# A mixed-layer kernel (FFT filter, then soft MoE): the first DFT stage as float32 on four 64x64 tiles, over sums and differences of token pairs

## The chip, the core and the metric

The kernel runs on one core of one Trainium2 chip. The core has a matmul engine (TensorE, PE in the profile, with its weight loads as PEld), a vector engine (VectorE, DVE), a scalar engine (ScalarE, ACT), GpSimd (POOL) and SyncE (SP), which in this kernel issues every DMA. The metric is the device time of one execution in microseconds (us). Three timed executions of the kernel before took 419.14, 420.32 and 425.69 us; the median, 420.32 us, is the time before.

## The reference

The input is 8 sequences of 2496 tokens with 256 channels. Each channel is filtered in the frequency domain, and the result goes through a soft mixture of experts (8 experts of 4 slots each).

```python
X = np.fft.rfft(x, axis=1)                      # x: (8, 2496, 256)
y = np.fft.irfft(X * (filt_r + 1j * filt_i)[None], n=2496, axis=1)
x = y.reshape(19968, 256)
logits = x @ phi                                # (19968, 32)
d = softmax(logits, axis=0)                     # dispatch, over the tokens (its sum + 1e-9)
slot_input = d.T @ x                            # 32 x 256
for e in range(8):                              # four slots each
    slot_out[e] = np.maximum(slot_input[e] @ w1[e], 0) @ w2[e]
c = softmax(logits, axis=1)                     # combine, over the slots
return c @ slot_out
```

## The kernel before

The DFT of 2496 points is split as 39 x 64 (`N1`, `N2`). A first stage takes, for each of the 64 residues, a DFT over 39 tokens and keeps 20 of the 39 frequencies (`NT`), since x is real. A second stage multiplies by the 64-point matrices.

**First stage** (`split_x`, `s1_unit`). x is laid out on the host so that 3 residues of 39 tokens (117 rows, `KR`) lie on the partitions. One unit is two such columns, 512 numbers wide; a batch has 11 units (`NH`). A unit of batches 1 to 7 is split into a high and a low part: ACT rounds x to `xh` (line 297), POOL makes `xl = x - xh` (line 298), and PE adds three matmuls in the format float32r into one PSUM bank (line 311), with the block-diagonal matrix `w1h` or `w1l`, 117 rows by 120 columns (3 residues x 20 frequencies x real and imaginary part). Batch 0 takes one float32 matmul for each unit (line 308). The PSUM pool `ps_s1` has two banks, one unit each. The result is copied to SBUF as `at` by ACT (line 315; in batch 0 every second by DVE, line 313) and stored to DRAM (`a_dram`, line 319).

**Second stage** (`load_ash`, `x_unit`). The store to DRAM and the load back (`ash`, line 332) turn the layout: 64 residues x real and imaginary part come to lie on the 128 partitions. A batch has ten slots of two frequencies: four float32 matmuls of 128 columns (line 342), the filter on DVE and POOL (lines 355 to 359), and two slots later four transposes (line 369) and their copy `y` (line 371); the logits' spectrum follows (line 380).

**Chains** (`chain`). When the last batch of a group is through, a chain of smaller steps turns the logits' spectrum back into logits (lines 413 to 460), takes the softmax over tokens (line 492), transforms the weights (lines 509 to 557) and adds up the slots' inputs (line 584). Two of its steps are issued with each slot.

**Order.** The loop over 80 slots (8 batches x 10) issues, for slot n, the load of `ash` five slots ahead (`ASH`), the second stage of n, the first-stage units that `at_slot` gives to n (those of the next batch, five slots early, `AHEAD`), the transposes of n - 2 and two chain steps. From this the framework's scheduler makes a fixed order for each engine. SP has one queue, in which a DMA that waits for a buffer, for a copy or for the eighth DMA before it holds up everything behind. Before slot 0 lie batch 0's first stage and the loads of the filter tables, spread by the string `STEPS`. After the slots come the last chains, the experts (lines 819 to 845) and the output (`blocks`, lines 908 and 917).

## Time and profile before

The profiled execution took 419.54 us; its span, from the first to the last instruction, was 417.4 us at a mean granted TensorE clock of 0.967.

| engine | busy us | share of the span |
|---|---|---|
| PE, matmuls | 370.9 | 89% |
| PE, weight loads | 284.1 | 68% |
| DVE | 271.2 | 65% |
| ACT | 218.3 | 52% |
| POOL | 201.6 | 48% |
| DMA queue of SP | 106.26 MB moved | 79.4% of 16 engines |

Busy time is the union of an engine's instructions; matmuls are pipelined, so a busy PE isn't PE at its peak. The stages lie one behind the other: until 39 us the front (x of batch 0, tables, its first stage), from 39 to 292 us the 80 slots, with first-stage units until 234 us, until 340 us the last chains, then the experts and the output. Shares mean little over the whole span, so the stages are read apart.

### The profile page before, as it was taken

To read this page: it belongs to the slowest core of one execution; us is meant where nothing else is said; L and a number is where in the kernel's file an instruction comes from. 1 tells how busy PE (TensorE), PEld (TensorE's weight loads), DVE (VectorE), ACT (ScalarE), POOL (GpSimd) and SP (SyncE) were. 2 spreads that over 40 slices of the span, in tenths; PEclk is the share of its full clock that TensorE was granted. 3 is DMA by queue.
4 is the path that set the end of the run, shared out by engine and by line. 5 is a ranking of instruction groups with operands and counts; after the bars stand their busy time and mean duration, and the time that the engine had idled before them with its cause. 6 is when DMAs were issued, how large, how long until landed. Compare 5 with 4: busy or idle time off the path is not lost.

```text
span 417.4 us, 12612 instructions
## 1 busy us (share of the span) xinstructions
PE 370.9 (89%) x5049; PEld 284.1 (68%) x5049; DVE 271.2 (65%) x495; ACT 218.3 (52%) x474; POOL 201.6 (48%) x234
## 2 busy tenths in 40 slices
PE   8667898999999899999997999998998889989940
PEld 3235676888878787887886678888676634688830
DVE  1341672987889973878999475899259522487740
ACT  2376557675667845676685434444255411376630
POOL 0027669798769564967786225666021200433100
PEclk9688999999999999999999999999999999999985
DMA  8999999999969978797996543442169899199996
GB/s 215 232 302 292 311 303 326 344 303 339 295 197 347 300 223 236 215 269 193 276 285 207 169 152 85 121 130 77 53 201 379 282 296 321 49 415 410 417 417 279
DMA packets 61084, 107.07 MB, mean 256 GB/s; under 512 B 6046, under 2 KB 37662, under 8 KB 58850
## 3 DMA queue, kind: packets, MB, share of 16 engines
q1 hardware_dynamic: 61026, 106.26, 79.4%
q8 instruction: 40, 0.66, 0.6%
q14 instruction: 18, 0.15, 0.1%
HBM read 63.50 MB, written 42.74 MB: 255 GB/s over the span
## 4 chain that ended last, share of the span: by engine, by line
PE 59%; DMA 18%; DVE 11%; ACT 4%; issue 3%; SPq 1%; POOL 1%; ACTq 0%; DVEq 0%; POOLq 0%
PE x L342 14%; PE s L311 7%; DMA xt<-in_x 7%; PE t L369 6%; PE out L908 5%; PE s L584 4%; DMA ash<-a_dram 4%; PE l L380 4%; DMA out<-ob 3%; PE v L426 3%; PE dt L540 2%; DVE t L356 2%; PE lg L453 2%; PE s L308 2%; PE h L819 2%
## 5 line engine op out<-in xcount | busy, mean ns | idle before, releaser
L298 POOL TENSOR_TENSOR xl<-xt,xh 117x512 fp32r<-117x512 f32 x77 | 102.6, 1345 | 54.2 <-ACT xh L297 49.6
L342 PE MATMUL x<-b_t,ash 128*128 128x128 f32 x640 | 90.0, 281 | 7.7 <-DMA ash<-a_dram 4.6
L342 PEld LDWEIGHTS x<-b_t,ash 128*128 128x128 f32 x640 | 79.8, 191 | 18.8 <-issue 7.0
L359 POOL TENSOR_TENSOR yt<-yt,t 128x256 f32<-128x256 f32 x80 | 65.8, 825 | 40.2 <-DVE t L356 30.9
L355 DVE TENSOR_TENSOR yt<-x,fr_t 128x512 f32<-128x512 f32 x80 | 54.7, 684 | 39.6 <-PE x L342 36.1
L297 ACT CAST xh<-xt 117x512 fp32r<-117x512 f32 x77 | 46.9, 623 | 36.7 <-DMA xt<-in_x 12.3
L371 ACT COPY y<-t 128x512 f32<-128x512 f32 x80 | 46.5, 591 | 34.5 <-PE t L369 28.7
L315 ACT COPY at<-s 120x512 f32<-120x512 f32 x83 | 48.3, 586 | 23.1 <-PE s L308 11.3
L356 DVE TENSOR_TENSOR t<-x,fi_t 128x512 f32<-128x512 f32 x80 | 54.3, 679 | 0.0
L369 PE MATMUL t<-cst_t,yt 128*128 128x128 f32 x320 | 48.5, 276 | 1.3 <-issue 0.7
L358 DVE TENSOR_TENSOR yt<-yt,t 128x256 f32<-128x256 f32 x60 | 44.8, 756 | 0.8
L369 PEld LDWEIGHTS t<-cst_t,yt 128*128 128x128 f32 x320 | 37.3, 141 | 8.5 <-issue 3.6
L311 PE MATMUL s<-xh,w1h 117*120 117x512 f32 x77 | 36.1, 469 | 3.9 <-ACT xh L297 3.6
L908 PE MATMUL out<-so_h,st 32*128 32x256 f32 x312 | 30.2, 300 | 3.8 <-ACT st L862 3.1
L311 PE MATMUL s<-xl,w1h 117*120 117x512 f32 x77 | 32.7, 424 | 0.2
L311 PE MATMUL s<-xh,w1l 117*120 117x512 f32 x77 | 31.3, 406 | 0.0
L358 POOL TENSOR_TENSOR yt<-yt,t 128x256 f32<-128x256 f32 x20 | 16.2, 808 | 30.6 <-DVE t L356 24.2
L917 DVE COPY ob<-out 128x512 f32<-128x512 f32 (+1 forms) x40 | 25.2, 672 | 6.3 <-PE out L908 5.1
L908 PEld LDWEIGHTS out<-so_h,st 32*128 32x128 f32 x312 | 24.0, 183 | 6.7 <-ACT st L862 3.5
L908 PE MATMUL out<-so_l,st 32*128 32x256 f32 x312 | 28.0, 277 | 0.0
L917 ACT COPY ob<-out 128x512 f32<-128x512 f32 (+1 forms) x40 | 21.3, 580 | 11.4 <-PE out L908 9.1
L380 PE MATMUL l<-yt,phi_t 128*32 128x128 f32 x640 | 26.1, 278 | 1.3 <-ACT y L371 1.2
(116 smaller groups left out, 552.9 us busy)
## 6 DMA issues: line engine op xcount, KB each, us to landing
ash<-a_dram SPq DMA_DIRECT2D x80, 256.0 KB
a_dram<-at SPq DMA_DIRECT2D x80, 240.0 KB
xt<-in_x SPq DMA_DIRECT2D x40, 448.0 KB
out<-ob SPq DMA_DIRECT2D x17, 1024.0 KB
w<-in_w SPq DMA_DIRECT2D x64, 256.0 KB
out<-ob SPq DMA_DIRECT2D x5, 512.0 KB
xt<-in_x SPq DMA_DIRECT2D x8, 224.0 KB
c_dram<-lg SPq DMA_DIRECT2D x2, 643.5 KB
```

Of the source, the lines that this page charges most:

```text
L297: act.copy(xh, xs)
L298: pool_e.tensor_tensor(out=xl, in0=xs, in1=xh.bitcast(F32), op=ALU.subtract)
L311: pe.matmul(ps, w, xx, start=(n == 0), stop=(n == 2))
L315: act.copy(at, ps)
L342: pe.matmul(ps[:, 2 * k + dh].rearrange("q r c -> q (r c)"), ash[:, k, dh * P : (dh + 1) * P], b_t[:, t0 + k, :], start=True, stop=True,)
L355: dve.tensor_tensor(out=yt, in0=ps, in1=frv, op=ALU.mult)
L356: dve.tensor_tensor(out=t2, in0=ps[:, :, ::-1, :], in1=fiv, op=ALU.mult)
L358: add.tensor_tensor(out=yt[:, :, 1, :], in0=yt[:, :, 1, :], in1=t2[:, :, 1, :], op=ALU.add)
L359: pool_e.tensor_tensor(out=yt[:, :, 0, :], in0=yt[:, :, 0, :], in1=t2[:, :, 0, :], op=ALU.subtract)
L369: pe.transpose(pt[:, k, dh, :], yt[:, c % 2, 2 * k + dh].rearrange("q r c -> q (r c)"), ident)
L371: act.copy(y, pt.rearrange("k p h d -> k p (h d)"))
L908: nc.tensor.matmul(prs[k][:, mm, :], st[q, n // 2, c0 : c0 + P], (so_h, so_l)[n % 2][q, :], start=(n == 0), stop=(n == 3),)
```

## The change

Every token pair s and 39 - s enters the real part through its sum and the imaginary part through its difference. The host now lays x out as 20 + 19 tokens side by side, the second in reverse; two residue groups (`h`) lie on partitions 0 to 63 and 64 to 127, 60 of 64 rows used, with zeros in the rest. `fold_x` makes the sums `e` (on DVE for batch 0, on POOL after it) and, in place, the differences (always POOL). The real part is a 60 x 60 matrix times `e`, the imaginary part a 60 x 60 matrix times the difference, both in float32. `s1_unit` issues four matmuls on the four quarters of the array: rows by `h`, columns by real or imaginary part. A unit now is two of the old ones; a batch has 6 (`NU`), the last half as wide. Its PSUM tile has two banks, one for each `h`, and `ps_s1` holds one such tile. The rounding on ACT and the split on POOL are gone. Each unit has two copies and four stores of 60 partitions, where two old units had two stores of 120. `a_dram` holds all real parts ahead of the imaginary ones, so the second stage's matrices have their rows reordered, and the copies of `minv` and `u` now turn that order on the way (strided reads). x is loaded in one DMA of 128 partitions where there were two (112 and 5). Four x tiles of one unit are held (`XB`), instead of three of two old units, and six half-unit `at` tiles (`AB`) instead of five of a unit.

```diff
-XC = 4
-XB = 3
-AB = 5
+XB = 4
+AB = 6
...
-        for lo, hi in ((0, RX), (RX, KR)):
-            sp.dma_start(t[lo:hi, 0:n, :], x[b, lo:hi, i0 : i0 + n, :])
-        xts[b, c] = t
+    def load_x(b, u):
         pool = x0p if b == 0 else proda
+        t = pool.tile([P, 2, 2, DIM], F32, tag="xt", name=f"xt{b}_{u}", bufs=6 if b == 0 else XB)
+        n = min(2, NH - 2 * u)
+        sp.dma_start(t[:, 0:n], x[b, :, 2 * u : 2 * u + n])
+        xts[b, u] = t
...
-        xh = proda.tile([KR, 2, DIM], F32R, tag="xh", name=f"xh{b}_{u}", bufs=3)
-        xl = proda.tile([KR, 2, DIM], F32R, tag="xl", name=f"xl{b}_{u}", bufs=3)
-        act.copy(xh, xs)
-        pool_e.tensor_tensor(out=xl, in0=xs, in1=xh.bitcast(F32), op=ALU.subtract)
-        xhl[b, u] = xh, xl
+    def fold_x(b, u):
+        n = min(2, NH - 2 * u)
+        xt = xts.pop((b, u))
+        e = proda.tile([P, 2, DIM], F32, tag="e", name=f"e{b}_{u}", bufs=3)
+        eng = dve if b == 0 else pool_e
+        eng.tensor_tensor(out=e[:, 0:n], in0=xt[:, 0:n, 0], in1=xt[:, 0:n, 1], op=ALU.add)
+        pool_e.tensor_tensor(out=xt[:, 0:n, 1], in0=xt[:, 0:n, 0], in1=xt[:, 0:n, 1], op=ALU.subtract)
+        folds[b, u] = e, xt[:, :, 1]
...
-            for n, (w, xx) in enumerate(((w1h, xh), (w1l, xh), (w1h, xl))):
-                pe.matmul(ps, w, xx, start=(n == 0), stop=(n == 2))
-        if b == 0 and u % 2 == 1:
-            dve.tensor_copy(at, ps)
-        else:
-            act.copy(at, ps)
+        ps = ps_s1.tile([P, 2, 2, DIM], F32, tag="s1", name=f"s1_{b}_{u}")
+        for h in range(2):
+            half = slice(FP * h, FP * h + FP)
+            for r in range(2):
+                pe.matmul(ps[FP * r : FP * r + FP, h, 0:n], wf_t[half, r], eo[r][half, 0:n], start=True, stop=True)
+        for h in range(2):
+            at = proda.tile([P, 2, DIM], F32, tag="at", name=f"at{b}_{u}_{h}", bufs=AB)
+            if b == 0 and h == 1:
+                dve.tensor_copy(at[:, 0:n], ps[:, h, 0:n])
+            else:
+                act.copy(at[:, 0:n], ps[:, h, 0:n])
+            for r in range(2):
+                src = at[FP * r : FP * r + PK * NF]
...
-        at_slot.setdefault((b - 1) * CPB + min(u, CPB - 1) - AHEAD, []).append((b, u))
+        at_slot.setdefault((b - 1) * CPB + u * CPB // NU - AHEAD, []).append((b, u))
```

On PE, late in batch 0's slots, the first two units of batch 2 stood apart, each with two matmuls first and the third, on `xl`, some groups later (`s1_2_0` is batch 2, unit 0; `x` and `t` are second-stage matmuls and transposes of a batch and slot, `l` the logits):

```order
L311 MATMUL s1_2_0_576<-xh2_0_512,w1h_74 120x512
L311 MATMUL s1_2_0_576<-xh2_0_512,w1l_75 120x512
L342 MATMUL x_0_7_654<-b_t_79,ash0_7_416 128x128 x4
L311 MATMUL s1_2_1_624<-xh2_1_558,w1h_74 120x512
L311 MATMUL s1_2_1_624<-xh2_1_558,w1l_75 120x512
L369 MATMUL t_0_5_671<-cst_t_78,yt_0_4_522 128x128 x4
L413 MATMUL ltr_0_0_1234<-cst_t_78,lt_0_491 128x128
L380 MATMUL l_0_2_678<-yt_0_4_522,phi_t_81 32x128 x8
L311 MATMUL s1_2_0_576<-xl2_0_513,w1h_74 120x512
```

Of the changed kernel the same units, each now two old ones:

```order
L310 MATMUL s1_2_0_570<-e2_0_522,wf_t_72 64x512
L310 MATMUL s1_2_0_570<-xt2_0_377,wf_t_72 64x512
L310 MATMUL s1_2_0_570<-e2_0_522,wf_t_72 64x512
L310 MATMUL s1_2_0_570<-xt2_0_377,wf_t_72 64x512
L374 MATMUL t_0_7_738<-cst_t_74,yt_0_6_615 128x128 x4
L418 MATMUL ltr_0_0_1194<-cst_t_74,lt_0_501 128x128
L385 MATMUL l_0_3_745<-yt_0_6_615,phi_t_77 32x128 x8
L310 MATMUL s1_2_1_620<-e2_1_554,wf_t_72 64x512
```

The four matmuls of a unit stand together; between two units lie 13 other matmuls at this place, and the second unit needs the PSUM tile of the first.

On SP's queue, where batch 1's first stage ends and batch 1's second stage loads its first `ash`, before:

```order
L319 DMA a_dram1_288<-at1_9_528 120x2x256
L321 DMA a_dram1_288<-at1_10_535 120x256
L322 DMA a_dram1_288<-at1_10_535 40x256
L761 DMA cst_t_78<-in_cst 128x697
L281 DMA xt2_3_562<-in_x 112x1024
L281 DMA xt2_3_562<-in_x 5x1024
L319 DMA a_dram2_575<-at2_0_577 120x2x256
L319 DMA a_dram2_575<-at2_1_625 120x2x256
L281 DMA xt2_4_651<-in_x 112x1024
L281 DMA xt2_4_651<-in_x 5x1024
L332 DMA ash1_0_549<-a_dram1_288 128x512
```

and in the changed kernel:

```order
L284 DMA xt2_3_525<-in_x 128x1024
L327 DMA a_dram1_317<-at1_5_0_486 60x256 x2
L327 DMA a_dram1_317<-at1_5_1_490 20x256 x2
L284 DMA xt2_4_557<-in_x 128x1024
L337 DMA ash1_0_545<-a_dram1_317 128x512
L323 DMA a_dram2_569<-at2_0_0_575 60x2x256 x2
L323 DMA a_dram2_569<-at2_0_1_579 60x2x256 x2
L337 DMA ash1_1_600<-a_dram1_317 128x512
```

Each store is two DMAs (x2), real and imaginary part. The load of `ash`, which waits until the stores have landed, has moved up: one DMA lies between it and the last store, where there were seven.

More of the change, by code (lines that the diff above doesn't have):

```diff
@@ L55 @@
 PR = 2
-FB = 1
 WM = 3
@@ L200, in x_layout @@
 def x_layout(x):
-    s2 = np.array([[run_of(i, j) for i in range(NI)] for j in range(PK)])
-    a = x.reshape(BATCH, N1, N2, DIM)[:, :, s2]
-    return np.ascontiguousarray(a.transpose(0, 2, 1, 3, 4)).reshape(BATCH, KR, NI, DIM)
+    a = np.zeros((BATCH, 2, FP, NH, 2, DIM), x.dtype)
+    xs = x.reshape(BATCH, N1, N2, DIM)
+    for h in range(2):
+        for j in range(PK):
+            s2 = [run_of(2 * i + h, j) for i in range(NH)]
+            rows = slice(j * NF, j * NF + NF)
+            a[:, h, rows, :, 0] = xs[:, 0:NF, s2]
+            a[:, h, j * NF + 1 : j * NF + NF, :, 1] = xs[:, : N1 - NF : -1, s2]
+    return a.reshape(BATCH, P, NH, 2, DIM)
 def out_rows():
@@ L228, in fft_soft_moe @@
     scr = ctx.enter_context(tc.tile_pool(name="scr", bufs=3, space=DRAM))
-    ps_s1 = ctx.enter_context(tc.tile_pool(name="ps_s1", bufs=2, space=PSUM))
     ps_x = ctx.enter_context(tc.tile_pool(name="ps_x", bufs=2, space=PSUM))
@@ L232, in fft_soft_moe @@
     ps_c = ctx.enter_context(tc.tile_pool(name="ps_c", bufs=2, space=PSUM))
-    w1q_t = const.tile([KR, QP], F32, name="w1q_t")
-    nc.sync.dma_start(w1q_t, w1q)
-    w1h = const.tile([KR, QP], F32R, name="w1h")
-    w1l = const.tile([KR, QP], F32R, name="w1l")
-    nc.vector.tensor_copy(w1h, w1q_t)
-    nc.vector.tensor_tensor(out=w1l, in0=w1q_t, in1=w1h.bitcast(F32), op=ALU.subtract)
+    ps_s1_cm = tc.tile_pool(name="ps_s1", bufs=1, space=PSUM)
+    ps_s1 = ps_s1_cm.__enter__()
+    wf_t = const.tile([P, 2, FP], F32, name="wf_t")
+    nc.sync.dma_start(wf_t, wf)
     cst_t = const.tile([P, CST.shape[1]], F32, name="cst_t")
@@ L301, in s1_unit @@
+    a_dram = {}
+    folds = {}
+    def fold_x(b, u):
[6 more added lines that the diff above has]
+        folds[b, u] = e, xt[:, :, 1]
     def s1_unit(b, u):
         if u == 0:
-            a_dram[b] = scr.tile([N2, QR, DIM], F32, tag="a_dram", name=f"a_dram{b}")
@@ L304, in s1_unit @@
-        xh, xl = xhl.pop((b, u))
-        ps = ps_s1.tile([QP, 2, DIM], F32, tag="s1", name=f"s1_{b}_{u}")
-        at = proda.tile([QP, 2, DIM], F32, tag="at", name=f"at{b}_{u}", bufs=AB)
-        if xl is None:
-            pe.matmul(ps, w1q_t, xh, start=True, stop=True)
-        else:
-            for n, (w, xx) in enumerate(((w1h, xh), (w1l, xh), (w1h, xl))):
-                pe.matmul(ps, w, xx, start=(n == 0), stop=(n == 2))
-        if b == 0 and u % 2 == 1:
-            dve.tensor_copy(at, ps)
-        else:
-            act.copy(at, ps)
@@ new lines, in s1_unit @@
+        for h in range(2):
+            half = slice(FP * h, FP * h + FP)
+            for r in range(2):
+                pe.matmul(ps[FP * r : FP * r + FP, h, 0:n], wf_t[half, r], eo[r][half, 0:n], start=True, stop=True)
+        for h in range(2):
+            at = proda.tile([P, 2, DIM], F32, tag="at", name=f"at{b}_{u}_{h}", bufs=AB)
[3 more added lines that the diff above has]
+                act.copy(at[:, 0:n], ps[:, h, 0:n])
+            for r in range(2):
+                src = at[FP * r : FP * r + PK * NF]
+                if n == 2:
+                    rows = a_dram[b][r, 0 : 4 * PK * (NU - 1)].rearrange(
+                        "(u i h j) t d -> u h (j t) i d", i=2, h=2, j=PK
+                    )
+                    sp.dma_start(rows[u, h], src)
+                else:
+                    k0 = 4 * PK * u + PK * h
+                    m = min(PK, N2 - k0)
+                    sp.dma_start(a_dram[b][r, k0 : k0 + m].rearrange("k t d -> (k t) d"), src[0 : m * NF, 0])
@@ L395, in chain @@
         wk = late_pool[0] if g == NG - 1 else work
-        banks = [(ps_s1, "s1"), (ps_x, "x"), (ps_t, "t")][:PR] if g == NG - 1 else [(ps_c, "c")]
+        banks = [(ps_o, "s1"), (ps_x, "x"), (ps_t, "t")][:PR] if g == NG - 1 else [(ps_c, "c")]
         turn = [0]
@@ L692, in fft_soft_moe @@
     be_t = x0p.tile([P, 2 * P + 2 * NT], F32, name="be_t", bufs=1)
-    split_x(0, 0)
-    for u in range(NH):
-        if u + 1 < NH:
-            split_x(0, u + 1)
+    fold_x(0, 0)
+    for u in range(NU):
+        if u + 1 < NU:
+            fold_x(0, u + 1)
         else:
-            split_next(-AHEAD)
+            fold_next(-AHEAD)
         s1_unit(0, u)
+        step()
         step()
@@ L809, in fft_soft_moe @@
     nc.vector.tensor_copy(sit, psi)
-    po = ps_s1.tile([P, DIM], F32, tag="s1", name="slot_out")
+    po = ps_o.tile([P, DIM], F32, tag="s1", name="slot_out")
     hts = []
```

76 lines of the change are left out of this document (36 added, 40 removed).

## The prediction

> **What bounds the kernel now.** I read the stages first. Each row of this table gives, for one stretch, the busy time of the five engines (instructions in brackets), the granted clock, the busy share of the DMA engines and GB/s.
>
> ```profile
> core 0: us, PE busy (x) PEld busy (x) DVE busy (x) ACT busy (x) POOL busy (x), PEclk, DMA share, GB/s
> 0.00:39.00 39.00, 27.70 (x63) 13.54 (x63) 10.20 (x28) 19.10 (x44) 8.90 (x16) 0.82 0.90 254
> 39.00:100.00 61.00, 57.44 (x502) 45.92 (x503) 42.28 (x70) 40.01 (x81) 49.62 (x47) 1.00 1.02 322
> 100.00:140.00 40.00, 38.45 (x572) 31.47 (x570) 35.81 (x57) 26.84 (x56) 29.07 (x27) 1.00 0.94 290
> 140.00:235.00 95.00, 92.56 (x1274) 74.71 (x1278) 75.63 (x120) 60.22 (x129) 63.15 (x57) 1.00 0.81 238
> 235.00:292.00 57.00, 54.04 (x915) 45.20 (x908) 43.81 (x79) 23.00 (x51) 28.09 (x38) 1.00 0.39 116
> ```
>
> PE looks full from 39 us on, but up to 100 us the DMA engines are full too (1.02). The chain that ended last says who leads. These are its shares by line, first for 39 to 100 us, then its longest pieces there, then the shares for 100 to 235 us.
>
> ```profile
> by line: DMA ash<-a_dram 26.5%; PE x L342 17.9%; DMA xt<-in_x 10.3%; DMA a_dram<-at 10.2%; PE s L311 9.5%; PE t L369 8.2%; issue 4.4%; DVE t L356 3.9%; PE l L380 3.8%; DVE yt L355 3.4%; SPq L281 3.2%; POOL xl L298 2.1%; DVE yt L358 2.0%; AC
> ...
> 57.36 6.25 DMA a_dram<-at
> 66.75 4.72 DMA ash<-a_dram
> 93.41 5.36 DMA ash<-a_dram
> ...
> by line: PE x L342 22.4%; PE s L311 18.6%; PE t L369 9.1%; DMA xt<-in_x 8.6%; PE l L380 6.2%; PE lg L453 3.6%; PE s L584 3.2%; PE dt L540 3.2%; issue 2.6%; PE v L426 2.4%; DVE d L491 2.3%; PE v L446 1.8%; ACT xh L297 1.8%; PE u L526 1.6%; D
> ```
>
> So until 100 us transfers lead (47% of that chain), and from 100 to 235 us PE does, with the first stage's matmuls (L311) on 18.6% of 135 us, 25.1 us. After 235 us the first stage is over. That makes two sums: PE's saving counts from 100 to 235 us, what the change adds to the DMA counts before.
>
> **PE: the first stage's price.** These pieces of the chain show matmuls at their pace, with start and length.
>
> ```profile
> 109.28 0.70 PE s L311 x3
> ...
> 106.84 0.65 PE l L380 x16
> ...
> 263.53 0.86 PE lg L453 x2
> ...
> 264.83 0.89 PE x L342 x8
> ...
> 343.52 1.85 PE h L819 x16
> ```
>
> An old unit, three float32r matmuls of 512 columns, takes 0.70 us; the two that a new unit replaces take 1.40. A float32 matmul of 512 columns on the whole array takes 0.86/2 = 0.43 us (L453). L819 has float32 matmuls of 512 columns on four column strips: 16 in 1.85 us, so four take 0.46 us, and the strips run side by side. That row strips do so too is seen at the output's matmuls, 32 rows by 128 columns, float32r, 256 wide (start, length, count):
>
> ```profile
> 365.06 0.39 PE L908 MATMUL out<-so_h,st 32*128 32x256 f32 x4
> 365.18 0.40 PE L908 MATMUL out<-so_l,st 32*128 32x256 f32 x4
> 365.30 0.39 PE L908 MATMUL out<-so_h,st 32*128 32x256 f32 x4
> 365.41 0.39 PE L908 MATMUL out<-so_l,st 32*128 32x256 f32 x4
> ```
>
> Four start every 0.12 us, what one of 256 columns takes alone (0.70/3/2). No row shows rows and columns split at once, so the new unit lies between 0.46 us (four side by side) and 4 x 0.43 = 1.72 us (one after another). I take the lower end, since each axis alone runs at full overlap. A burst on strips also pays for its ends: L380's 16 matmuls of 128 columns would take four times 0.43/4, or 0.43 us, and take 0.65, 0.2 more. A new unit is then 0.65 us against 1.40. The Trainium skill (TensorEngine Tiling (Array Packing), Key Properties) says that a change of the tiling mode drains the engine. The trace agrees as far as this 0.2 us goes; without a drain the unit would be 0.46 us.
>
> On the chain of 100 to 235 us, 25.1 us of L311 become 25.1 x 0.65/1.40 = 11.7 us: **13.4 us** fewer. All of it can't come out. DVE is busy for 35.81 + 75.63 = 111.4 of these 135 us, and the DMA for 0.94 x 40 + 0.81 x 95 = 114.6. Room is left, but at over 85% everywhere waits begin to meet; I count three quarters, **-10 us** (bounds -4 and -16, the latter at 0.46 us a unit). Before 100 us L311 has 9.5% of 61 us, 5.8 us, of which 3.1 would go; transfers lead there, so I count **-1 us**.
>
> **The operands on ACT, POOL, DVE.** These are the groups' rows, with busy time and the mean in ns of one.
>
> ```profile
> L298 POOL TENSOR_TENSOR xl<-xt,xh 117x512 fp32r<-117x512 f32 x77 | 102.6, 1345 | 54.2 <-ACT xh L297 49.6
> ...
> L359 POOL TENSOR_TENSOR yt<-yt,t 128x256 f32<-128x256 f32 x80 | 65.8, 825 | 40.2 <-DVE t L356 30.9
> ...
> L297 ACT CAST xh<-xt 117x512 fp32r<-117x512 f32 x77 | 46.9, 623 | 36.7 <-DMA xt<-in_x 12.3
> L371 ACT COPY y<-t 128x512 f32<-128x512 f32 x80 | 46.5, 591 | 34.5 <-PE t L369 28.7
> L315 ACT COPY at<-s 120x512 f32<-120x512 f32 x83 | 48.3, 586 | 23.1 <-PE s L308 11.3
> L356 DVE TENSOR_TENSOR t<-x,fi_t 128x512 f32<-128x512 f32 x80 | 54.3, 679 | 0.0
> ```
>
> ACT loses 77 casts, 46.9 us, and keeps its copies, now of 128 rows as those of y (L371); being idle half the time it gives none of this to the end. POOL trades 11 subtractions a batch (14.8 us) for ten of 512 numbers and two of 256 (10 x 1.345 + 2 x 0.825 = 15.1 us). The fold is two POOL steps in a row (2.7 us) where cast and subtraction took 0.6 + 1.3, but it stands a slot ahead of its matmuls, and POOL is busy 49.62 of 61 us at its fullest. I count nothing; without that cover, 0.8 us for each of 42 units would show. In batch 0, six sums on DVE (near 0.7 us each by L356) and six differences on POOL go where both are nearly idle, 0 to 39 us. PE's six units there, each with a copy before the next (0.65/0.82 + 0.6 = 1.4 us, 8.4 in all), take longer than eleven of 0.43/0.82 (5.8 us); the front's DMA, busy for 0.90 of it, hides the 2.6 us, which I keep for the range.
>
> The copies of u and minv only change their stride:
>
> ```profile
> L519 ACT COPY u<-u 128x240 f32<-128x240 f32 (+5 forms) x30 | 8.3, 346 | 1.1 <-PE u L509 0.9
> ```
>
> No row shows the other stride; between nothing and twice this (8.3 us over the run, off the chain mostly) I take nothing, as the count of numbers is the same, and keep 3 us for the range.
>
> **DMA.** Two DMA views bear on this: the packets of 60 to 100 us, then the issues on SP's queue over the run (min/median/max ns).
>
> ```profile
> DMA packets 8344, 13.07 MB, mean 327 GB/s; under 512 B 773, under 2 KB 5054, under 8 KB 8340
> ...
> L281 SPq DMA_DIRECT2D xt<-in_x x96: 262/333/1290, 1.2 to 214.8; - x96
> ...
> L319 SPq DMA_DIRECT2D a_dram<-at x80: 317/344/1505, 13.7 to 234.0; - x80
> ```
>
> x grows from 117 to 128 rows of 22 KB, by 0.25 MB a batch. Until 100 us 39 x 254 + 61 x 322 GB/s = 29.5 MB moved, with some 3.3 batches of x among them: 0.8 MB more at 322 GB/s is **+2.5 us**. The low end is nothing, since the extra transfers of five rows fall away. SP issues 40 DMAs a batch (6 of x, 24 stores, 10 of `ash`) instead of 34 at 0.34 us: 13.6 us of some 31, hidden. The load of `ash` moved up on SP and holds what is behind it, the next batch's stores, until the last stores land; the same loads wait 4.7 and 5.4 us now (66.75, 93.41), so this moves a wait and adds none. In the front all the filter tables now stand ahead of the first `ash`; they fill the same queue either way, and I take nothing (up to +4 us: 1.3 MB more ahead of it at 322 GB/s).
>
> **Sum.** The profiled execution took 419.5 us (span 417.4), 0.8 below the median of 420.3. 419.5 - 10 - 1 + 2.5 = **411 us**.
>
> **The rivals.**
>
> *The gain is used up by the others.* DMA leads to 100 us and is at 0.94 until 140; if PE's saving only lets it wait for x and `ash` there and for DVE (35.81 of 40 us) later, the -10 is the low end, -4, and the front pays 2 to 4 us: 416 to 422, say 419. For: three engines over 80%. Against: 18.6% of the chain is a matmul that gets shorter. A half overlap (two by two, 0.92 us a unit) lands here too.
>
> *The one PSUM tile.* `ps_s1` had two banks for two units; now a unit's matmuls must wait until both copies of the unit before, both on ACT (2 x 0.586 = 1.17 us), are done, and everything on PE waits behind them. Between two units stand few other matmuls (13 at one place, five of 0.89/8 and eight of 0.65/16, 0.9 us). If ACT comes to its copies late and a unit waits more than 0.75 us, the saving is gone; at 1.3 us, about 0.55 us is lost for each of 42 units, 23 us, partly under the DMA before 100 us: 14 us of it, with the +2.5, gives 436; at 1.0 us, 428. Against: ACT is freed of 77 casts and the units lie in different slots. The Trainium skill (TensorEngine Tiling (Array Packing), PSUM Bottleneck) says that tiling speeds up TensorE but not the evacuation of PSUM, and advises to use both ScalarE and VectorE; here ACT does it alone after batch 0. By that rule this case decides; the trace so far has PE waiting for such a copy 0.3 us in all, and its weight loads 1.9.
>
> ```profile
> PE s L311 <- ACT at L315: 0.3, 1, 0.3
> ...
> PEld s L311 <- ACT at L315: 1.9, 5, 0.7
> ```
>
> *The four quarters don't overlap.* Then the change doesn't do on the array what it is laid out for: 1.72 us against 1.40 is 23% more on 25.1 + 5.8 us, +7; in batch 0, at the low clock (0.82), six units of 4 x 0.43/0.82 = 2.1 us and a copy of 0.6, 16 us, replace eleven of 0.52, 5.8 us: +10, of which I let the DMA hide half; with the +2.5, 434.
>
> **How the numbers follow.** Forecast (403 to 416) 0.49; gain used up (416 to 422) 0.25; one PSUM tile (422 to 436) 0.15; no overlap (430 to 440) 0.07; better than 403, if the waits before 100 us shrink as well, 0.04. The range 402 to 429 holds the first two, about half of the third and a little of the last, 0.83. Its lower end is the sum at -16 with nothing for the DMA (402.5), its upper end the PSUM case at a wait of 1.0 us. What this measurement can tell from no change is about 2%, 8.4 us: faster means below 412, slower above 428.7. The forecast lies just below 412, but its chance isn't split evenly at that line, as most of its terms were taken short of their full size: 0.42 of its 0.49 go to faster, 0.07 to the same. So faster 0.42 + 0.04 = 0.46; the same 0.07 + 0.25 + 0.03 of the PSUM case = 0.35; slower 0.12 + 0.07 = 0.19.
>
> **What would show it.** In the profile of the changed kernel: the four matmuls of a unit start within 0.1 us and end within about 0.6 us (right) or follow each other by 0.43 (wrong). The chain of 100 to 235 us has the first stage at under 10% and DMA and DVE higher. The first-stage units end near 225 us instead of 234. PE waiting for the copies of `at` stays under 5 us in all; some 20 us would be the PSUM case. Until 100 us the second stage has come as far as before, within 3 us. If the chain after 235 us gets longer, or the output comes no earlier though the first stage ends earlier, the sum is wrong where it lets 10 us run through to the end.

## The result, and the profile after

The changed kernel takes **434.6 us** (median of 4 runs, 432.8 to 435.8) beside 420.7 us before on the same chip: a ratio of 1.034, 95% interval 1.028 to 1.040. It is slower by 3.4%, where 411 us was forecast, and it lies above the forecast's range (402 to 429). In the times and ratios below, a run more than 1.5% above the fastest of its kernel is left out as slow: one in xb5 (842.5 us, the one that was profiled), two each in xb3 and halves, one each in full, nofold, st2d4 and st2nofold. The profiled execution took 432.8 us, its span 430.9 us, against 419.5 and 417.4 before.

The stages of the changed kernel, in the columns of the first table of the prediction (stretch, busy time of PE, weight loads, DVE, ACT and POOL, granted clock, busy share of the DMA engines, GB/s):

```profile
core 0: us, PE busy (x) PEld busy (x) DVE busy (x) ACT busy (x) POOL busy (x), PEclk, DMA share, GB/s
0.00:39.00 39.00, 21.73 (x78) 7.49 (x78) 14.75 (x33) 13.57 (x33) 19.04 (x22) 0.69 0.88 281
39.00:100.00 61.00, 51.47 (x482) 35.40 (x483) 37.07 (x63) 25.63 (x54) 43.92 (x44) 0.94 0.91 288
100.00:140.00 40.00, 37.47 (x486) 25.33 (x484) 29.25 (x49) 18.12 (x39) 30.16 (x31) 1.00 0.91 302
140.00:235.00 95.00, 85.38 (x1335) 62.37 (x1338) 75.30 (x124) 43.90 (x96) 56.60 (x53) 0.95 0.71 219
235.00:292.00 57.00, 56.33 (x815) 42.93 (x808) 38.41 (x71) 23.56 (x49) 30.00 (x38) 1.00 0.58 172
```

PE and the DMA engines, which led before, are no busier until 235 us than they were. PE's busy time fell from 57.44 to 51.47 us in the second stretch and from 92.56 to 85.38 in the fourth; the DMA engines' share fell too, from 1.02 to 0.91 and from 0.81 to 0.71. Both wait more. The chain that ended last says for whom, by line from 39 to 100 us, and then from 100 to 235 us:

```profile
by line: DMA xt<-in_x 27.5%; POOL e L297 17.1%; DMA ash<-a_dram 13.5%; POOL xt L298 13.4%; PE x L347 9.9%; issue 6.8%; POOL yt L364 5.2%; DMA a_dram<-at 2.9%; PE s L310 1.7%; PE l L385 1.5%; DVE yt L360 1.1%; DVE t L361 1.0%; SPq L337 0.9%;
```
```profile
by line: PE x L347 19.3%; PE s L310 12.2%; PE t L374 9.8%; DMA xt<-in_x 9.3%; PE l L385 5.6%; DMA ash<-a_dram 3.8%; PE lg L458 3.8%; PE s L592 3.2%; DVE d L496 3.1%; POOL e L297 2.8%; DVE lg L615 2.8%; PE u L514 2.2%; POOL xt L298 2.1%; PE 
```

Until 100 us the leaders are the loads of x and the two steps of POOL's fold (`e` and the difference, 30.5% together; the prediction had counted the fold at nothing). After 100 us the first stage's matmuls hold 12.2% of the chain where they held 18.6%.

These waits are new, or larger than before:

```profile
POOL e L297 <- PE s L310: 17.8, 9, 8.4
PEld s L310 <- DVE at L314: 14.9, 5, 3.5
POOL e L297 <- DMA xt<-in_x: 14.3, 11, 3.2
PEld t L374 <- POOL yt L364: 13.8, 12, 1.8
PE u L514 <- ACT u L524: 9.4, 2, 5.0
SPq L284 <- PE s L310: 24.5, 18, 3.9
```

The last row is SP's queue: a load of x (L284) waits for the matmuls of an earlier unit, since the x tile now serves as the place of the difference and is held until then. Everything behind it on SP waits too.

To see where the time was lost I followed one thing through all kernels: the start of the first multiplication by the filter in each batch (DVE, `yt<-x,fr_t`), which marks how far the second stage has come. For batch 2, before and after:

```profile
97.00 0.69 DVE L355 TENSOR_TENSOR yt<-x,fr_t 128x512 f32<-128x512 f32 x1 [1.46 <-PE x L342]
```
```profile
102.10 0.69 DVE L360 TENSOR_TENSOR yt<-x,fr_t 128x512 f32<-128x512 f32 x1 [0.99 <-PE x L347]
```

| us, start in the trace | before | after |
|---|---|---|
| batch 0 | 40.4 | 44.6 |
| batch 1 | 72.7 | 73.7 |
| batch 2 | 97.0 | 102.1 |
| batch 3 | 129.3 | 138.4 |
| batch 4 | 170.7 | 185.1 |
| batch 6 | 247.4 | 258.3 |
| last slot | 304.5 | 316.9 |
| end of span | 417.4 | 430.9 |

So 9 us are lost by batch 3, 14 by batch 4, and 11 to 14 stay to the end. The loss lies in batches 1 to 3. (The slots of the kernel before thus run to some 305 us, not to 292 as said with the stages above.)

Two numbers of the prediction fall at once. One unit in the changed kernel, on PE's timeline:

```profile
123.73 0.64 PE L310 MATMUL s<-e,wf_t 64*64 64x512 f32 x1
123.74 0.64 PE L310 MATMUL s<-xt,wf_t 64*64 64x512 f32 x1
123.75 0.64 PE L310 MATMUL s<-e,wf_t 64*64 64x512 f32 x1
123.75 0.64 PE L310 MATMUL s<-xt,wf_t 64*64 64x512 f32 x1
124.21 0.59 PE L310 MATMUL s<-e,wf_t 64*64 64x512 f32 x1
124.22 0.59 PE L310 MATMUL s<-xt,wf_t 64*64 64x512 f32 x1
124.23 0.59 PE L310 MATMUL s<-e,wf_t 64*64 64x512 f32 x1
124.23 0.59 PE L310 MATMUL s<-xt,wf_t 64*64 64x512 f32 x1
```

The four quarters do start within 0.02 us of each other. But each float32 matmul leaves two records, half a microsecond apart: the unit's four matmuls are eight records, and it takes 1.02 us ("123.80 1.02 PE s L310 x8" in the chain), not 0.65. The same is seen before, where the eleven float32 units of batch 0 leave 22 records:

```profile
L308 PE MATMUL s<-xt,w1q_t x22: 590/598/1061, 6.9 to 24.6; 117*120 117x512 f32 x22
```

### The profile page after: what moved, and what is told of

Its sections match the earlier page's. It is cut to its first block, busy times and chain, and to the rows that moved or that the text cites. A ratio compares the mean times of both kernels' runs of the same rounds, so it can differ in the third digit from the quotient of the medians.

```text
span 430.9 us, 12815 instructions
## 1 busy us (share of the span) xinstructions
PE 365.9 (85%) x5180; PEld 259.3 (60%) x5180; DVE 270.7 (63%) x500; ACT 180.5 (42%) x404; POOL 210.1 (49%) x247
## 4 chain that ended last, share of the span: by engine, by line
PE 53%; DMA 20%; DVE 9%; POOL 7%; ACT 3%; SPq 3%; issue 2%; DVEq 0%; POOLq 0%; ACTq 0%
PE x L347 12%; DMA xt<-in_x 10%; PE out L922 7%; PE t L374 6%; PE s L310 5%; PE s L592 4%; DMA w<-in_w 4%; PE l L385 4%; DMA ash<-a_dram 3%; POOL e L297 3%; POOL xt L298 3%; PE v L431 2%; PE dt L548 2%; PE lg L458 2%; PE u L514 2%
## 5 line engine op out<-in xcount | busy, mean ns | idle before, releaser
L316 ACT COPY at<-s 128x512 f32<-128x512 f32 (+1 forms) x90 | 45.6, 553 | 78.4 <-PE s L310 47.3
L297 POOL TENSOR_TENSOR e<-xt 128x512 f32<-128x512 f32 (+1 forms) x42 | 52.2, 1244 | 35.9 <-PE s L310 17.8
L310 PE MATMUL s<-e,wf_t 64*64 64x512 f32 (+1 forms) x192 | 56.8, 627 | 13.2 <-DVE at L314 13.0
L298 POOL TENSOR_TENSOR xt<-xt 128x512 f32<-128x512 f32 (+1 forms) x48 | 59.7, 1246 | 15.0 <-DVE e L297 12.4
L374 PE MATMUL t<-cst_t,yt 128*128 128x128 f32 x320 | 51.6, 285 | 5.5 <-POOL yt L364 5.5
L310 PE MATMUL s<-xt,wf_t 64*64 64x512 f32 (+1 forms) x192 | 56.3, 626 | 0.0
L363 DVE TENSOR_TENSOR yt<-yt,t 128x256 f32<-128x256 f32 x60 | 36.3, 623 | 0.6
L922 PE MATMUL out<-so_h,st 32*128 32x256 f32 x312 | 32.2, 311 | 4.1 <-ACT st L876 3.1
L922 PE MATMUL out<-so_l,st 32*128 32x256 f32 x312 | 30.2, 289 | 0.0
L310 PEld LDWEIGHTS s<-e,wf_t 64*64 64x64 f32 x192 | 11.7, 140 | 28.8 <-DVE at L314 14.9
L385 PE MATMUL l<-yt,phi_t 128*32 128x128 f32 x640 | 26.8, 281 | 0.1
L931 ACT COPY ob<-out 128x512 f32<-128x512 f32 (+1 forms) x40 | 21.4, 579 | 12.6 <-PE out L922 10.8
```

The costliest lines, as they stand in the source:

```text
L297: eng.tensor_tensor(out=e[:, 0:n], in0=xt[:, 0:n, 0], in1=xt[:, 0:n, 1], op=ALU.add)
L298: pool_e.tensor_tensor(out=xt[:, 0:n, 1], in0=xt[:, 0:n, 0], in1=xt[:, 0:n, 1], op=ALU.subtract)
L310: pe.matmul(ps[FP * r : FP * r + FP, h, 0:n], wf_t[half, r], eo[r][half, 0:n], start=True, stop=True)
L363: add.tensor_tensor(out=yt[:, :, 1, :], in0=yt[:, :, 1, :], in1=t2[:, :, 1, :], op=ALU.add)
L374: pe.transpose(pt[:, k, dh, :], yt[:, c % 2, 2 * k + dh].rearrange("q r c -> q (r c)"), ident)
L922: nc.tensor.matmul(prs[k][:, mm, :], st[q, n // 2, c0 : c0 + P], (so_h, so_l)[n % 2][q, :], start=(n == 0), stop=(n == 3),)
```

## The experiments

The theories at the start were these. *Holding*: x tiles that come free only with the matmuls delay the loads, and the supply runs dry. *Queue*: SP issues too many DMAs. *Matmul*: the unit is dearer than priced. *POOL*: the fold in front of the matmuls costs. Later came *PSUM* (the single tile) and *order* (any edit shifts the instructions, and that alone costs). Ratios are to the kernel before on the same chip.

**More or fewer x tiles.** `XB` is 4 in the change. One kernel (xb5) has 5, and 32 y tiles instead of 34 (`YB`) to make room; the other (xb3) has 3. The edit of the first:

```diff
-XB = 4
+XB = 5
...
-YB = 34
+YB = 32
```

> One more x tile (five instead of four; two y tiles fewer to make room). Supply theory (x is held until its matmuls, so its next load comes late, and 48 to 120 us of the chain is load, sum, difference, load): 5 to 8 us faster than the changed kernel, ratio to before about 1.02. Queue theory (SP has too many DMAs to issue, above all in the front): no change, 1.034. Matmul theory (a unit takes 1.02 us, not 0.65, and that is the whole story): no change, 1.034.

> One x tile fewer (three instead of four). Supply theory: 10 us or more slower than the changed kernel, ratio to before 1.06 or more. Queue theory: within 3 us of it, 1.03 to 1.04. Matmul theory: no change, 1.034.

With five tiles 440.9 us (1.052, 1.046 to 1.059); with three 440.3 us (1.048, 1.038 to 1.057; two runs, 437.3 and 443.3). Taking a tile away costs some 6 us, though the interval overlaps that of the change a little (1.028 to 1.040), so the supply of x seems to matter. The run with five says nothing on it, since two y tiles had to go; what that costs was not tried.

**The difference in a tile of its own.** With three x tiles, as in the run before; besides the moment of release, one `at` tile fewer (five instead of six) differs from it.

```diff
-XB = 4
-AB = 6
+XB = 3
+AB = 5
...
-        pool_e.tensor_tensor(out=xt[:, 0:n, 1], in0=xt[:, 0:n, 0], in1=xt[:, 0:n, 1], op=ALU.subtract)
-        folds[b, u] = e, xt[:, :, 1]
+        d = proda.tile([P, 2, DIM], F32, tag="d", name=f"d{b}_{u}", bufs=3)
+        pool_e.tensor_tensor(out=d[:, 0:n], in0=xt[:, 0:n, 0], in1=xt[:, 0:n, 1], op=ALU.subtract)
+        folds[b, u] = e, d
```

> The difference goes into a tile of its own (three of them), so an x tile is free once POOL has read it and not only after its matmuls; to make room, three x tiles instead of four and five half-unit at tiles instead of six. To be held against the run with three x tiles (1.048). Holding theory (SP stands 24 to 33 us waiting for first-stage matmuls to free x, with stores and ash behind it): that wait falls below 10 us and the time to 1.02 to 1.03. POOL theory (two POOL steps a unit, in POOL's order ahead of the second stage's own step, set the pace): no gain, 1.045 or more. Queue theory (number of issues): 1.045.

434.1 us (1.032, 1.024 to 1.040). SP's wait, with three tiles held until the matmuls:

```profile
SPq L284 <- PE s L310: 28.0, 21, 3.9
```

and with the same three, free after the fold:

```profile
SPq L284 <- POOL d L299: 11.0, 8, 3.0
```

Against three held tiles some 6 us come back, with intervals that overlap. Holding seems to cost where tiles are scarce; but the kernel is then just as slow as the changed one with four, so this alone doesn't bring it to the old time.

**The matmul's price.** Two matmuls on the whole array (block-diagonal weights) in place of four quarters:

```diff
...
-        for h in range(2):
-            half = slice(FP * h, FP * h + FP)
-            for r in range(2):
-                pe.matmul(ps[FP * r : FP * r + FP, h, 0:n], wf_t[half, r], eo[r][half, 0:n], start=True, stop=True)
+        for r in range(2):
+            pe.matmul(ps[:, r, 0:n], wf_t[:, r], eo[r][:, 0:n], start=True, stop=True)
...
```

> The same sums and differences by two float32 matmuls on the whole array (128 rows by 128 columns, block diagonal) instead of four on quarters, so 2 x 0.86 = 1.72 us a unit instead of 1.02; PSUM tile, copies and stores as many as in the changed kernel. If PE's time decides, 42 x 0.7 = 29 us more on PE and some 15 us or more in the end, ratio to before 1.07. Supply and queue theories: PE has slack until 140 us, 3 to 8 us more, 1.04 to 1.055.

433.9 us (1.035, 1.028 to 1.041): the same as with quarters, although a unit now takes 1.72 us of PE instead of 1.02, 29 us more over 42 units. One thing softens this: the granted clock is higher with whole-array matmuls (1.00 instead of 0.94 from 39 to 100 us, 0.98 instead of 0.95 from 140 to 235). On the changed kernel's busy time there (51.47 and 85.38 us) that is worth some 6 us of PE, by estimate, so the weight added is nearer 23 us. It still does not show: what a unit costs on PE does not decide the time of the changed kernel. The gain that the prediction counted at 10 us can't appear, because PE has that time to spare.

**No fold, PE adds.** Eight quarter matmuls a unit accumulate what the fold did on POOL; the second of these kernels also has five x tiles (no `e` tiles, so there is room).

```diff
...
-        for h in range(2):
-            half = slice(FP * h, FP * h + FP)
-            for r in range(2):
-                pe.matmul(ps[FP * r : FP * r + FP, h, 0:n], wf_t[half, r], eo[r][half, 0:n], start=True, stop=True)
+        for k in range(2):
+            for h in range(2):
+                half = slice(FP * h, FP * h + FP)
+                for r in range(2):
+                    w = wf_t[half, r + (r == 1 and k == 1)]
+                    pe.matmul(ps[FP * r : FP * r + FP, h, 0:n], w, xk[half, 0:n, k], start=(k == 0), stop=(k == 1))
...
```

> No sums or differences on POOL and DVE: PE makes them by accumulating, eight matmuls on quarters for a unit (about 2.04 us instead of 1.02), everything else as in the changed kernel. POOL theory: POOL loses some 110 us of work, PE gains 43 us where it had slack; ratio to before 1.00 to 1.02. Holding theory: x is still held until its matmuls, the fold's 2.6 us fall out of the way from load to matmul; 1.02 to 1.03. Matmul theory: slower than the changed kernel, 1.07 or more.

> The same with five x tiles instead of four (the room is that of the sums, nothing else changes). Holding theory: SP waits less for first-stage matmuls and the time falls by 4 us or more against the run with four. POOL and matmul theories: no difference between the two.

459.1 us (1.089, 1.083 to 1.095) and 460.7 us (1.092, 1.086 to 1.098). From 140 to 235 us PE is full:

```profile
140.00:235.00 95.00, 94.35 (x1252) 60.93 (x1254) 61.08 (x113) 39.91 (x86) 18.16 (x22) 1.00 0.68 206
```

With 1.88 us a unit, or 2.9 where the scheduler puts it in two pieces, PE is the bound, and neither POOL's relief nor another x tile can show. I had taken the first as a sign against POOL; it is none, as the later runs without a fold tell.

**Half the stores.** Both halves of a unit go into one tile, and real and imaginary part are stored in one DMA each: 14 stores a batch instead of 24. A second kernel (st2act) issues these on ACT's queue, with `act.dma_start` in the last line.

```diff
-            at = proda.tile([P, 2, DIM], F32, tag="at", name=f"at{b}_{u}_{h}", bufs=AB)
+        at = proda.tile([P, 2, 2, DIM], F32, tag="at", name=f"at{b}_{u}", bufs=AB // 2)
...
+                    "(u g j) t d -> u (j t) g d", g=4, j=PK
...
+                sp.dma_start(rows[u], src)
```

> Both halves of a unit go into one tile and are stored by two DMAs instead of four (three such tiles). Queue theory: the first load of ash is issued near 34 us instead of 39.8, 5 to 8 us faster than the changed kernel, ratio to before about 1.02. Supply theory: 0 to 3 us faster (x loads wait less behind stores), 1.03. Matmul theory: no change, 1.034.

> The run with two stores a unit (1.023), but the stores are issued on ACT's queue, behind ACT's own copies, and no longer on SP's. Queue and holding theories both say that what stands behind a blocked SP is what costs: 5 us or more off the run with two stores, ratio to before 1.01 or less, with SP's waits for x no longer delaying stores. POOL theory: no change, 1.02.

On SP 430.0 us (1.023, 1.016 to 1.031), 4.6 us off the change, though the two intervals overlap a little. On ACT's queue 439.3 us (1.045, 1.036 to 1.053): SP is relieved, but its loads of x and `ash` then wait for matmuls and for the stores, now issued by ACT:

```profile
SPq L284 <- PE s L310: 63.3, 34, 6.2
SPq L338 <- DMA a_dram<-at: 23.5, 13, 6.8
```

**The stores alone, on the kernel before.** Each full store is split in two DMAs of 60 partitions, as in the change. Nothing else is touched.

```diff
-            dma(a_dram[b][k0 : k0 + 2 * PK].rearrange("(i j) q d -> (j q) i d", j=PK), at)
+            rows = a_dram[b][k0 : k0 + 2 * PK].rearrange("(i j) q d -> (j q) i d", j=PK)
+            for lo in (0, QP // 2):
+                dma(rows[lo : lo + QP // 2], at[lo : lo + QP // 2])
```

> The kernel before, with one thing of the change: every store of a full unit is two DMAs of 60 partitions instead of one of 120 (ten issues more a batch on SP's queue; the last unit's two stores as they were). Nothing else is touched, so x tiles come free after the split as before. Queue theory (too many issues of 0.4 us stand in SP's queue ahead of the loads): 425 to 428, as merging the stores of the changed kernel in pairs took 4.6 us off it. Holding theory (x tiles that come free only with the matmuls): no change, 419 to 422.

**433.5 us** (1.030, 1.024 to 1.036): 12.4 us for 80 more issues, nearly the whole loss of the change, with the old matmuls, casts and x tiles. Its second stage falls behind where that of the changed kernel does: batch 3 starts at 138.2 us (138.4 in the change, 129.3 before), batch 4 at 184.5 (185.1 and 170.7). The bytes are the same; the transfers got worse all the same:

```profile
39.00:100.00 61.00, 50.70 (x419) 40.32 (x419) 36.48 (x61) 33.27 (x67) 42.70 (x41) 0.98 0.92 277
```

The DMA share is 0.92 where it was 1.02, and 277 GB/s where it was 322: as in the changed kernel (0.91 and 288). An issue of half a store doesn't take half the time on SP, but more than that of a whole one (344 ns at the median before; min/median/max here):

```profile
L321 SPq DMA_DIRECT2D a_dram<-at x160: 315/408/1499, 13.4 to 248.3; - x160
```

In the changed kernel it is the same number:

```profile
L323 SPq DMA_DIRECT2D a_dram<-at x160: 315/408/1667, 13.9 to 257.4; - x160
```

The scheduler had answered the split with another order on the other engines too (on PE 193 rows differ), so the order could have been the cause. Three runs bear on this.

**Issues without another order, order without other work.** The split in batches 3 to 7 only, which leaves PE's order as it was word for word (bs3, below); in batches 1 to 7 (bs1, the same with `b >= 1`); and no split, but the first stage six slots ahead instead of five (bah6).

```diff
...
+            w = QP // 2 if b >= 3 else QP
+            for lo in range(0, QP, w):
+                dma(rows[lo : lo + w], at[lo : lo + w])
```
```diff
-AHEAD = 5
+AHEAD = 6
```

> The kernel before with each full store split in two DMAs of 60 partitions in batches 3 to 7 only: 50 issues more on SP's queue, and PE's instructions in exactly the order they had. If extra issues cost time by themselves wherever they stand, five batches out of eight bear five eighths of the 12.4 us: 427 to 429. If they cost it only where the transfers lead (until about 140 us, one of these batches), 422 to 424. If the order is what costs, no change: 419 to 422.

> The same split in batches 1 to 7 (70 issues more); on PE 87 rows of the order move, where with batch 0's stores split too 193 moved. If the issues cost the time: 430 to 433. If it is batch 0's split and the order that comes with it: 420 to 425.

> The kernel before with the first stage one slot further ahead of the second (six slots instead of five). Same instructions, same transfers, another order: 358 rows of PE's order move. Order theory (an order that differs costs up to 3% whatever the edit): 426 to 434. Issue theory: within 2% of before, 417 to 425.

The split in batches 3 to 7 takes 424.3 us (1.009, 1.006 to 1.012), in batches 1 to 7 432.2 us (1.027, 1.020 to 1.034); the other order alone 422.2 us (1.005, 1.001 to 1.008). So another order costs 2 us (0.1 to 0.8%), as far as one such order can say. The issues cost: 50 of them in batches 3 to 7 4.1 us, 0.08 us each; the 20 more of batches 1 and 2 another 7.9 us, 0.39 us each, which is the time that SP takes for one. So the added issues of the stretch that transfers lead cost far more than the later ones. (Batch 0's ten add 0.5 us, within the noise.) Whether SP's time for the issue does it, or the smaller transfers in flight, these runs don't tell apart. SP's queue was not out of time: from 39 to 100 us its waits add up to 19.0 us with the split, 13.0 of them for an earlier DMA to land (26.8 and 17.7 before), which speaks for the transfers. And 87 rows of PE's order moved with the split of batches 1 to 7, so part of the 7.9 us may be order.

**The loads of x alone, on the kernel before.** One DMA of 128 partitions (zeros in the last 11) in place of 112 and 5.

```diff
...
-        for lo, hi in ((0, RX), (RX, KR)):
-            sp.dma_start(t[lo:hi, 0:n, :], x[b, lo:hi, i0 : i0 + n, :])
+        sp.dma_start(t[:, 0:n, :], x[b, :, i0 : i0 + n, :])
...
```

> The kernel before with the x loads of the changed one: 128 partitions in one DMA (11 rows of zeros) instead of 112 and 5 in two, so 9% more bytes of x and six issues fewer a batch; the matmuls read the same 117 rows. By the bytes alone, as in the prediction: +2.5 us, 423. If SP's issues are what counts, six fewer a batch of 34 give back 3 to 6 us: 415 to 419. If any other order costs (463 rows of PE's order move): 426 to 434.

418.7 us (0.996, 0.993 to 0.999): a little faster. What the 9% more bytes of x cost, six issues fewer a batch pay back.

**No fold at all.** The matmuls of the changed kernel read the two loaded halves as they are; sums and differences are left out. Once with the stores as in the change, once with merged stores.

```diff
-        e = proda.tile([P, 2, DIM], F32, tag="e", name=f"e{b}_{u}", bufs=3)
-        eng = dve if b == 0 else pool_e
-        eng.tensor_tensor(out=e[:, 0:n], in0=xt[:, 0:n, 0], in1=xt[:, 0:n, 1], op=ALU.add)
-        pool_e.tensor_tensor(out=xt[:, 0:n, 1], in0=xt[:, 0:n, 0], in1=xt[:, 0:n, 1], op=ALU.subtract)
-        folds[b, u] = e, xt[:, :, 1]
+        folds[b, u] = xt[:, :, 0], xt[:, :, 1]
```

> The changed kernel without its sums and differences: the four matmuls read the two halves of the x tile as it was loaded (the sums and differences are left out of the computation). POOL loses 112 us of work and the 2.5 us between a landed x tile and its matmuls are gone, but the tile is still held until its matmuls are done, with four tiles as before. Holding theory in its narrow form (only the matmuls' late release counts): 430 to 436, no change. Fold theory (it is the two POOL steps in a row, 2.5 us at a time, between landing and use, that starve PE and lengthen the hold): 418 to 424. In between, 424 to 430: each has a part.

> The changed kernel with its stores merged in pairs (as in st2) and without the sums and differences (left out of the computation, as in nofold): the matmuls read the loaded halves, and the x tile is held until them. If stores (-4.6 us) and fold (-6.3 us) are separate and add up: 422 to 425. If one is only the cover of the other: 428 to 430. Below 419: with both gone the shorter matmuls show a gain.

426.6 us (1.015, 1.008 to 1.022), and with merged stores **421.8 us** (1.001, 0.996 to 1.006). The stores' 4.6 us and the fold's 8.0 us add up to 12.6; together they gave 12.8. With both gone the changed kernel is as fast as the one before, and no faster: its shorter matmuls show no gain even now. Its x tiles are still held until the matmuls (four of them), and SP waits for that even longer than the 24.5 us of the changed kernel, so with four tiles the hold is not what makes the difference:

```profile
SPq L284 <- PE s L306: 27.2, 19, 4.2
```

The stretch from 140 to 235 us has PE back at 91.26 us, and POOL's 56.60 down to 21.68:

```profile
140.00:235.00 95.00, 91.26 (x1478) 66.28 (x1473) 68.82 (x131) 47.88 (x106) 21.68 (x26) 0.98 0.79 248
```

How the fold cost there is seen in one place of the changed kernel. From 146.3 to 151.3 us PE stands still, as the last matmuls of `u` (L514) wait for ACT's copies of the first:

```profile
144.42 1.89 PE L514 MATMUL u<-cst_t,d 117*32 117x60 f32 x128
...
145.74 1.27 POOL L297 TENSOR_TENSOR e<-xt 128x512 f32<-128x512 f32 x1 [0.28 <-DMA xt<-in_x]
145.80 3.83 DVE L615 TENSOR_TENSOR lg<-lg,rm 117x704 f32<-117x704 f32 x2
...
147.08 1.80 POOL L298 TENSOR_TENSOR xt<-xt 128x512 f32<-128x512 f32 x1
...
149.72 0.79 ACT L616 ACTIVATE lg<-lg 117x704 f32<-117x704 f32 x1 [0.55 <-DVE lg L615]
...
150.56 1.18 ACT L524 COPY u<-u 128x240 f32<-128x240 f32 x4
...
151.26 1.45 PE L514 MATMUL u<-cst_t,d 117*32 117x60 f32 x45 [4.96 <-ACT u L524]
```

ACT's copies stand behind its exponentials of `lg`, these wait for DVE, and DVE's two subtractions take 3.83 us, as POOL folds at the same time. Without the fold the same two take 1.68 us:

```profile
142.82 1.68 DVE L612 TENSOR_TENSOR lg<-lg,rm 117x704 f32<-117x704 f32 x2
```

and PE's wait for these copies is gone, 1.2 us in all in place of 9.4:

```profile
PE u L511 <- ACT u L521: 1.2, 1, 1.2
```

That is 8 us of PE's waiting, in two places, about as much as the 8.0 and 8.2 us by which the runs differ (nofold from the change, st2nofold from st2). But this wait does not set the time by itself: with the difference in its own tile it is 5.5 us and the time 434.1. Whether the fold's cost goes this way is argued here, not shown; POOL's share of the chain before 100 us is the other way it can go.

**The PSUM tile taken apart.** Each half of a unit gets its own one-bank tile, two of them.

```diff
...
-        ps = ps_s1.tile([P, 2, 2, DIM], F32, tag="s1", name=f"s1_{b}_{u}")
+        ps = [ps_s1.tile([P, 2, DIM], F32, tag="s1", name=f"s1_{b}_{u}_{h}") for h in range(2)]
...
```

> The changed kernel with the PSUM tile of a unit taken apart: each half (two matmuls side by side) has its own one-bank tile, two of them, so that a half waits only for the copy of the same half of the unit before. PSUM theory (the single two-bank tile makes PE wait, 28 us of waits in the front): 428 or less. Holding theory: 432 to 437, the front at most 2 us earlier, since the waits in the front lie under the loading of x and tables. If the scheduler pulls the halves apart, each piece takes about 1.0 us and the run is slower, 437 to 445.

454.3 us (1.080, 1.073 to 1.087; two runs, 452.9 and 455.7). The scheduler now puts other work between the halves, and half a unit costs what a whole one does:

```profile
by line: PE s L310 29.1%; PE x L347 27.7%; PE t L374 12.5%; PE l L385 6.6%; DMA xt<-in_x 5.4%; DMA ash<-a_dram 3.8%; PE v L431 2.9%; SPq L323 2.2%; PE lg L458 1.9%; PE ltr L418 1.4%; POOL e L297 1.3%; POOL xt L298 1.3%; PE v L451 1.2%; issu
...
110.89 1.01 PE s L310 x4
...
138.67 1.00 PE s L310 x2
...
200.29 1.01 PE s L310 x6
```

Four, two or six records (the six stand in a later stretch of the same chain): a microsecond each. The two-bank tile keeps the four quarters together in most units, and so it is worth more than its waits cost.

**Both remedies, with nothing left out.** Merged stores and a tile for the difference, first with four x tiles, two each for sums and differences and two unit-sized `at` tiles (st2d4, below), then with three x tiles, two for sums, three for differences and three `at` tiles (st2d3d).

```diff
-AB = 6
+AB = 4
+DB = 2
...
+        d = proda.tile([P, 2, DIM], F32, tag="d", name=f"d{b}_{u}", bufs=DB)
...
```

> The changed kernel with the two remedies that helped alone: the stores of both halves of a unit in one DMA each for real and imaginary part (half the stores), and the difference in a tile of its own, so that an x tile comes free after POOL's fold. Four x tiles as in the changed kernel, two tiles each for sums and differences, two unit-sized tiles for the copies. If holding (about -6 us with three tiles) and the queue (-4.6 us) are separate causes and add up: 422 to 426. If the wait only moves on to the next tile in line (copies waiting for stores, two tiles): 429 to 434.

> The changed kernel with its stores merged in pairs and the difference in a tile of its own, so that an x tile is free after POOL's fold: three x tiles, two tiles for sums and three for differences, three unit-sized tiles for the copies as in st2. Nothing is left out. If the hold until the matmuls is what remains after the merged stores: 422 to 426. If the fold itself (POOL's 2.5 us a unit between landing and use) is: 428 to 432. With one x tile fewer the loads may start later and take it back: 432 to 438.

438.9 us (1.044, 1.038 to 1.050) and 434.2 us (1.030, 1.023 to 1.037). Neither beats the merged stores alone (430.0). Each of these runs gives up buffers for the tile of the difference; that this takes back what the early release gives is likely, but not shown.

**What stays open.** By batch 3 the changed kernel with merged stores and no fold is still at 137.5 us, 8 us behind (before: 129.3); it wins back 4 of them by the last slot (309.0 against 304.5). What keeps it behind early was not found: its stores are merged, its fold is gone, and the loads of x alone cost nothing. What the hold of four x tiles would cost on the kernel before was not tried.

## Why the prediction was wrong, point by point

- **The bound.** Right as read: transfers until 100 us, then PE. What did not follow is that PE's saving counts from 100 us on. With 29 us more of matmuls in 42 units (some 23 after the clock, full) the time did not move, and with stores and fold out of the way (st2nofold) it came back to that of the kernel before and not below it. So the step "on the chain of 100 to 235 us 25.1 us become 11.7" gave no gain: PE's share fell, and waits took its place, as in the rival *the gain is used up by the others*, only larger than it was priced.
- **The unit's price.** "A float32 matmul of 512 columns takes 0.86/2 = 0.43 us" was misread: the x2 of that row are two records of one matmul, which takes 0.86 us. The overlap was right (four starts within 0.02 us), the size was not: 1.02 us instead of 0.65. With it the term would have been 25.1 x 1.02/1.40 = 18.3 us, 6.8 fewer, of which three quarters are 5, not 10. The Trainium skill (FP8 and Floating Point Precision, TensorE Precision Notes) gives four passes for true float32; the rows agree, as 0.86 us is 3.7 times the 0.70/3 of a float32r matmul. L819's 16 records are eight matmuls in the same way, so that row had four side by side at 0.93 us, close to what came. The 0.2 us for the ends doesn't hang on the misreading: 0.86 + 0.2 = 1.06 us would have been near the 1.02. The eight logits matmuls between two units, priced at eight records, take 0.65 us and not half of it.
- **The DMA issues: a step that failed.** "40 DMAs a batch instead of 34 at 0.34 us: 13.6 us of some 31, hidden". The sum of the issues was compared with the batch's length, as if SP needed only to have time left. Splitting the stores costs 12.4 us on the old kernel, most of it in batches 1 and 2 (0.39 us for each added issue). That is not the stores' share of the 13.9 us here: in the changed kernel, merging them gave back 4.6. The six loads that fall away pay a little back (-1.6 us with bx128). The rule in the Trainium skill (DMA: Bandwidth & Descriptors, Rules for kernel authors) not to split a transfer into partition halves, as they share the same engines, would have warned; bsplit agrees with it.
- **The bytes of x.** +2.5 us was too much as a net term: with six issues fewer a batch, 0.4% faster.
- **POOL's fold: the larger of the two terms put at nothing.** The fold "stands a slot ahead of its matmuls", and "I count nothing". It costs 8.0 us (nofold) to 8.2 (st2nofold against st2), far below the 0.8 us a unit, 34 us, named for a lost cover. By which way is open: POOL slowing DVE after 140 us, or its 30.5% of the chain ahead of 100 us.
- **Holding x.** Not in the prediction at all. With three tiles it seems to cost some 6 us; with four it shows as SP's 24.5 us of waiting, but st2nofold waits 27.2 us and has the old time, so it is not the cause there.
- **The one PSUM tile.** PE did wait for copies for 13.0 us and its loads 14.9, over the 5 us named as the mark, but for DVE's copies, all in batch 0; for ACT's the weight loads waited 0.3 us (1.9 before). That rival gave the right time for another reason, by luck. Taking the tile apart cost 20 us. The advice of the Trainium skill (TensorEngine Tiling (Array Packing), PSUM Bottleneck) to share the evacuation between two engines does not bear here: after batch 0, where ACT copies alone, the weight loads wait for it 0.3 us in the changed kernel and the matmuls not at all.
- **The quarters don't overlap.** Wrong, as the starts show; and the case itself, 1.72 us a unit, gives 433.9 us. The 434 of that rival is luck too, as its terms were PE's time.
- **`ash`, the strided copies.** About right. PE waits for `ash` 6.7 us instead of 4.6, and a copy of `u` takes 354 ns instead of 346; that PE waits for these copies comes, in the place shown above, from what stands ahead of them on ACT.

```profile
PE x L347 <- DMA ash<-a_dram: 6.7, 3, 5.4
```
```profile
L524 ACT COPY u<-u 128x240 f32<-128x240 f32 (+5 forms) x30 | 8.5, 354 | 6.2 <-PE u L514 6.0
```

- **The front.** Batch 0's second stage starts 4.2 us later, the upper end of the +4 kept for the tables ahead of the first `ash`; batch 1 only 1.0 us later.
- **Smaller slips.** "At over 85% everywhere" is too high for DVE (111.4 of 135 us, 83%), and at 0.46 us a unit the bound is -16.9, not -16. Neither changes the outcome.
- **What would show it.** The chain's share under 10%: 12.2%. The first stage's end near 225 us: 261. The second stage as far as before at 100 us within 3 us: 5.1 us behind in batch 2. Each of these spoke against the forecast.

The forecast of faster rested on one term (-10) that could not appear, since PE's time in the first stage was not what the kernel waited for; and the two terms that did appear, stores (4.6 us) and fold (8.0), were counted at nothing because their engines had time to spare.

## What to carry to other kernels

An engine with idle time isn't free: where transfers led, splitting the same bytes into more DMAs on one in-order queue (SP here) cost 0.39 us for each, so count issues there, not only bytes, and test a split by making it alone on the old kernel. Before a row is used as a price, find out how many records an instruction leaves. And when a matmul gets cheaper, ask first, with a run that makes it dearer, whether its time is what the kernel waits for.
